# Two sliding-window attention and MLP layers on one core: three units project q, k, v by seven block products, the first unit's feed-forward reads its weights where they were split, attention takes four tokens per instruction

## The chip, the cores and the metric

One core of a Trainium2 chip runs the whole program. The metric is the device time of one execution in microseconds (us): the median of 3 runs of the kernel before is 1144.45 us (1144.21 to 1144.93).

## The reference

The input x is [1, 2048, 640] in fp32. Two layers follow each other with the same weights. Each does

```
x = x + A(layernorm(x));   x = x + B(layernorm(x))
A(y): q, k, v = y @ wqkv (640 x 1920), 32 heads of 20
      token s sees 8 keys: s, s-2, ..., s-14 (masked where negative)
      softmax over the 8 logits / sqrt(20), weighted sum of v, then @ wo (640 x 640)
B(y): h = gelu_tanh(layernorm(y) @ w1 + b1)   (640 x 1536)
      h @ w2 + b2                              (1536 x 640)
```

All products are to be as accurate as fp32; the kernel gets there by splitting each fp32 factor into two fp16 parts, high and low, and adding three of the four products (`PASS`).

## The kernel before

The 2048 tokens are cut into four *units* of 512 (even or odd tokens, first or second half; a partition holds four neighbouring tokens `t`). Two layers make eight units in order, 0 to 7. A unit goes through these stages:

- `layernorm(n, ..., twice=False)`: ScalarE (ACT) forms the statistics and the normalised row y, the high part and, on VectorE (DVE), the low part (L618); the DMA queue transposes each of the four tiles (`dma_transpose`) into a `yT` buffer.
- `qkv(n)`: 16 pieces (4 tokens x 4 head groups `g`), each 5 blocks of 128 rows x 3 passes = 15 matmuls of 480 columns (L648); ACT evicts each piece (L665) and SyncE (SP) writes it to a DRAM buffer `spill`.
- `fetch(G)` and `attention(G)`, 4 groups of heads per unit, G = 0 to 31: q, and k and v with their halo rows, come back from `spill`. DVE does the logits (products L732, sums over 20 L736), the softmax (L741 to L751, the exponential on ACT), the weighted sum (products L758, a tree of sums L766, L770). Each of L732, L736, L758, L766 is issued for two tokens at a time (`EH = 2`), and the two halves alternate in two `pr` buffers. GpSimd (POOL) splits the output for three groups of four, DVE for the fourth (L780).
- `project(n)`: 120 matmuls of 320 columns with wo (L805) onto the residual.
- `layernorm(n, ..., twice=True)`, then `mlp(at, b, t0, t1)`: for each of 12 blocks of 128 hidden columns 15 matmuls (L871), gelu and high part on ACT (L877, L880), low part on DVE (L882), 24 matmuls into five accumulators (L892). Both weight blocks are loaded again from DRAM (`mw`) for each part of `PARTS`.
- The last two units, 6 and 7, share one feed-forward in `pair()`, which already uses seven block products for eight: `sums_of_weights` (L1005, L1018, L1020) and `joint` (L952 to L978) make the sums of weights and of rows on DVE; L1108 and L1073 are its matmuls.

Before any feed-forward can start, all of w1 and w2 is read, split into fp16 parts (L475 on ACT, L476 on DVE) and stored in `mw` (`prep_m`, L517); `mlp` waits for all of it (`split_done`). Unit 0's feed-forward is cut into two parts of two tokens, `(0, 0, 2), (0, 2, 4)`, with matmuls of 256 columns in L871.

The order of all instructions on all engines is fixed when the program is built. `Plan` lists the operations with durations, priorities (lower first), what each needs and gives, and the buffers it uses (`SLOTS`; those in `ORDERED` go to their users in order), plays them through a model of the engines and the DMA queues, and emits each engine's instructions in the order that came out. At run time every engine works off its own list in that order and waits by semaphores. All DMAs but a few are issued by SP, in one such list.

Of the kernel before, what the change touches and what calls it, by code (L numbers as in the profile page):

```python
# [26 lines left out]
REST = D - BANK  # L27

# [3 lines left out]
M = 4  # L32
# [4 lines left out]
EH = 2  # L37

# [32 lines left out]
THROUGH = (("sa", 29),)  # L71
LOP = ((29, -460),)


class Plan:
# [23 lines left out]
    ORDERED = ("qk", "v", "yT", "o", "ohl", "c1", "c2", "hh", "h32", "ev", "raw")  # L99
# [191 lines left out]
def sliding_dilated_then_mlp_kernel(  # L291
# [25 lines left out]
    def many(pool, n, shape, dt, name):  # L317
# [3 lines left out]
             "sy": 4, "sa": 4, "sm": 2, "ln": 3, "ps": 3, "z": 2, "zh": 2, "raw": 2, **{f"acc{i}": 1 for i in range(5)}}  # L321
# [11 lines left out]
        "pr": many(sb, SLOTS["pr"], [P, EH, W, GC], FT, "pr"),  # L333
# [24 lines left out]
    blocks = [("o", k) for k in range(KD)] + [("m", f, i) for f in range(NF) for i in range(2)]  # L358
    through = {name: next(pool for pool, n in THROUGH if i < n) for i, name in enumerate(blocks)}
    split_done = [("lo", k) for k in blocks]  # L360

    def passed(pool):
        return [("lo", k) for k in blocks if through[k] == pool]
# [24 lines left out]
    for i, q in enumerate(("A12", "S1", "A22", "HL")):  # L388
# [4 lines left out]
        "pr": [("o", 2 * NU * NG - 1, a) for a in range(M // EH)] + [("done", 0, i) for i in range(M)],  # L393
# [84 lines left out]
    def prep_q(g, prio):  # L478
# [8 lines left out]
        for i in range(3):  # L487
# [3 lines left out]
            a, v = split(lambda i=i: wq[:, 0, :, g, i], lambda i=i: wq[:, 1, :, g, i], lambda i=i: st(i))  # L491
# [3 lines left out]
    def prep_rows(name, prio, src, hi, lo, use=()):  # L495
        key = (through[name], name)

        def load():
            st = tile_of(*key)
            w = src()  # L500
            nc.sync.dma_start(st.rearrange("p (k c) -> p k c", k=w.shape[1]) if len(w.shape) == 3 else st, w)

        dma(P * D * 4 / 1e3, prio, load, need=[("ev", 0, M - 1, 0)], give=[("st", name)], use=[key],
            packet=4 * P if name[0] == "m" and not name[2] else 4 * D)
        a, v = split(hi, lo, lambda: tile_of(*key))
        act(D, prio, a, need=[("st", name)], give=[("hi", name)], use=[key, *use])
        dve(D, next(p for n, p in LOP if blocks.index(name) < n), v, need=[("hi", name)], give=[("lo", name)], use=[key, *use])

    def prep_o(k, prio):
        prep_rows(("o", k), prio, lambda: A_wo[k * P:(k + 1) * P], lambda: wo[:, 0, k], lambda: wo[:, 1, k])  # L510
# [837 lines left out]
```

## Time and profile before

| | us |
|---|---|
| median of 3 runs | 1144.45 |
| span of the profiled execution | 1146.1 |
| TensorE (PE) matmuls busy in it | 1137.1 |
| DVE busy | 1038.4 |
| ACT busy | 606.6 |
| POOL busy | 113.2 |
| DMA, share of 16 engines | 70% |

The profiled execution's own time is known only by its span, from the first to the last instruction, which lies 1.65 us above the median. Busy time is the union of an engine's instructions; a stage can be bound by another engine than the whole. Matmuls overlap each other, so the time of a stretch of them is read from starts, or from the chain of work, and not from the duration of one.

### The profile page before, as it was taken

How to read it: one execution, taken by the hardware profiler on the slowest of the kernel's cores; microseconds unless marked ns; L12 is line 12 of the kernel's file. 1: busy time of each engine (PE TensorE's matmuls, PEld its weight loads, DVE VectorE, ACT ScalarE, POOL GpSimd, SP SyncE). 2: the span in 40 equal slices, each digit the busy share in tenths (PEclk: the TensorE clock that was granted, in tenths of full speed). 3: DMA queues.
4: the chain of work that ended last, by engine and by line, in shares of the span. 5: the costliest groups of instructions: out<-in, count | busy, mean ns of one | idle time of the engine just before them, and what ended most of it. 6: DMA issues, size and time to landing. Idle time of an engine off the chain costs nothing.

```text
span 1146.1 us, 17470 instructions
## 1 busy us (share of the span) xinstructions
PE 1137.1 (99%) x6812; PEld 628.4 (55%) x6812; DVE 1038.4 (91%) x1028; ACT 606.6 (53%) x1131; POOL 113.2 (10%) x94
## 2 busy tenths in 40 slices
PE   9999999999999999999999999999999999999998
PEld 6444446567565465546555555556455556555476
DVE  7999999999899999999999999999999993847972
ACT  6485336536365275734537662479347445657720
POOL 1010000211111102110112012012111000000000
PEclk9999999999999999999999999999999999999999
DMA  9999998978976477576655965569686555974201
GB/s 318 307 299 266 329 302 244 321 264 244 239 189 232 140 221 213 178 207 198 186 187 176 221 190 164 175 188 192 164 247 183 175 171 156 217 239 122 65 24 69
DMA packets 239791, 235.47 MB, mean 205 GB/s; under 512 B 139020, under 2 KB 195164, under 8 KB 239708
## 3 DMA queue, kind: packets, MB, share of 16 engines
q1 hardware_dynamic: 239708, 234.36, 69.9%
q8 instruction: 53, 0.87, 0.3%
q14 instruction: 30, 0.25, 0.1%
HBM read 157.55 MB, written 44.78 MB: 177 GB/s over the span
## 4 chain that ended last, share of the span: by engine, by line
PE 72%; DVE 3%; DMA 1%; issue 0%; ACT 0%; DVEq 0%
PE acc L892 18%; PE ps L871 17%; PE ps L648 17%; PE ps L805 10%; PE acc L1073 4%; PE ps L1108 3%; PE ps L1073 2%; DMA yT<-w 1%; DVE yT L1020 1%; DVE pr L1005 1%; PE acc L1108 1%; DVE wq L1194 0%; DVE wq L1182 0%; DVE v L1195 0%; DVE xf L1196 0%
## 5 line engine op out<-in xcount | busy, mean ns | idle before, releaser
L648 PE MATMUL ps<-wq,yT 128*128 128x480 f16 (+1 forms) x1950 | 391.0, 363 | 1.5 <-DMA yT<-w 1.1
L648 PEld LDWEIGHTS <-yT 128*128 128x128 f16 x1950 | 189.3, 98 | 200.8 <-DMA yT<-w 1.4
L892 PE MATMUL acc<-c,act 128*128 128x512 f16 (+1 forms) x1728 | 249.3, 299 | 2.3 <-DMA c<-mw 1.6
L871 PE MATMUL ps<-yT,c 128*128 128x512 f16 (+1 forms) x1260 | 247.8, 350 | 0.0
L892 PEld LDWEIGHTS <-act 128*128 128x128 f16 x1728 | 136.1, 98 | 108.8 <-issue 1.9
L871 PEld LDWEIGHTS <-c 128*128 128x128 f16 x1260 | 120.9, 98 | 107.3 <-DMA c<-mw 0.3
L732 DVE TENSOR_TENSOR pr<-qk 128x2560 f32<-128x2560 f32 x64 | 179.5, 2808 | 0.0
L758 DVE TENSOR_TENSOR pr<-sm,v 128x2560 f32<-128x2560 f32 x64 | 179.1, 2818 | 0.3
L736 DVE TENSOR_REDUCE sm<-pr 128x128 f32<-128x2560 f32 x64 | 179.2, 2801 | 0.0
L665 ACT ACTIVATE ev<-ps 128x480 f32<-128x480 f32 x128 | 72.6, 568 | 177.2 <-PE ps L648 157.5
L877 ACT ACTIVATE act<-ps,b 128x512 f32<-128x512 f32 (+1 forms) x84 | 52.4, 624 | 172.9 <-PE ps L871 170.2
L766 DVE TENSOR_TENSOR pr<-pr 128x640 f32<-128x640 f32 (+1 forms) x128 | 143.1, 1150 | 0.3
L805 PE MATMUL ps<-wo,yT 128*128 128x320 f16 x960 | 131.7, 299 | 0.0
L805 PEld LDWEIGHTS <-yT 128*128 128x128 f16 x960 | 93.8, 98 | 37.4
L780 POOL TENSOR_TENSOR ohl<-w,ohl 128x640 f16<-128x640 f32 x24 | 34.9, 1456 | 425.9 <-DVE pr L732 171.6
L882 DVE TENSOR_TENSOR act<-act 128x512 f16<-128x512 f32 (+1 forms) x84 | 51.0, 609 | 16.0 <-ACT act L880 15.9
L587 POOL TENSOR_TENSOR ln<-ln,half 128x2 f32<-128x2 f32 (+1 forms) x31 | 36.2, 1173 | 276.6 <-ACT ln L584 276.6
L625 POOL TENSOR_TENSOR xf<-xf,b 128x640 f32<-128x640 f32 x24 | 37.3, 1558 | 144.6 <-DVE pr L732 58.4
L880 ACT ACTIVATE act<-act 128x512 f16<-128x512 f32 (+1 forms) x84 | 47.5, 565 | 3.4 <-PE acc L892 1.5
L610 ACT ACTIVATE w<-xf,ln 128x640 f32<-128x640 f32 x53 | 47.5, 909 | 2.7 <-DVE w L618 2.1
L570 ACT ACTIVATE junk<-xf 128x640 f16<-128x640 f32 x57 | 41.8, 733 | 12.9 <-DVE xf L814 8.0
L618 DVE TENSOR_TENSOR w<-w,w 128x640 f16<-128x640 f32 x56 | 45.7, 830 | 2.1 <-ACT w L616 2.1
(200 smaller groups left out, 984.1 us busy)
## 6 DMA issues: line engine op xcount, KB each, us to landing
c<-mw SPq DMA_DIRECT2D x174, 320.0 KB, 3.6
spill<-ev SPq DMA_DIRECT2D x64, 480.0 KB, 3.6
qk<-spill SPq DMA_DIRECT2D x32, 880.0 KB, 6.0
v<-spill SPq DMA_DIRECT2D x32, 880.0 KB, 5.3
qk<-spill SPq DMA_DIRECT2D x32, 320.0 KB, 3.6
act<-in_B_w_dram SPq DMA_DIRECT2D x24, 320.0 KB, 4.9
mw<-c SPq DMA_DIRECT2D x24, 320.0 KB, 4.7
pr<-in_B_w_dram SPq DMA_DIRECT2D x24, 320.0 KB, 4.1
```

The costliest lines, as they stand in the source:

```text
L648: nc.tensor.matmul(ps, transposed(yk)[:, a * KD + k, t * P:(t + 1) * P], wq[:, b, k, g, i0:i1], start=first and j == 0, stop=last and j == ...
L665: act(3 * GC, -400 + n, lambda i=i, pk=pk, ek=ek: nc.scalar.activation(tile_of(*ek)[:, :, i], tile_of(*pk)[:, :3 * GC].rearrange("p (a c) ...
L732: nc.vector.tensor_mul(tile_of(*pk), w[:, HALO + m + t0:HALO + m + t0 + EH, None, :].to_broadcast([P, EH, W, GC]), windows(w, t0, [GC, W], ...
L736: dve(E, G - 0.7, lambda pk=pk, t0=t0: nc.vector.tensor_reduce(lg(t0, t0 + EH).rearrange("p t w h -> p (t w h)"), tile_of(*pk).rearrange(" ...
L758: nc.vector.tensor_mul(tile_of(*vk).rearrange("p t w (h d) -> p t (w h) d", d=DH), lg(t0, t0 + EH).rearrange("p t w h -> p t (w h)")[:, :, ...
L766: dve(EH * w * GC, G - 0.9, lambda vk=vk, w=w: nc.vector.tensor_add(tile_of(*vk)[:, :, 0:w], tile_of(*vk)[:, :, 0:w], tile_of(*vk)[:, :, w ...
L805: nc.tensor.matmul(tile_of(*pk)[:, :D // 2], transposed(yk)[:, a * KD + k, t * P:(t + 1) * P], wo[:, b, k, c * D // 2:(c + 1) * D // 2], s ...
L871: nc.tensor.matmul(tile_of(*pk)[:, :nt], tile_of(*ck)[:, a, k * P:(k + 1) * P], transposed(yk)[:, c * KD + k, t0 * P:t1 * P], start=i == 0 ...
L877: act(nt, -430, lambda pk=pk, h32=h32, e=e: nc.scalar.activation(tile_of(*h32)[:, :nt], tile_of(*pk)[:, :nt], AF.Gelu_apprx_tanh, bias=b1[ ...
L882: dve(nt, -1000, lambda h32=h32, hk=hk: nc.vector.tensor_sub(tile_of(*hk)[:, 1, :nt], tile_of(*h32)[:, :nt], tile_of(*hk)[:, 0, :nt]), nee ...
L892: nc.tensor.matmul(accs[k][:, c0:c0 + n], tile_of(*hk)[:, a, (i - t0) * P:(i - t0 + 1) * P], tile_of(*wk)[:, c, w0:w0 + n], start=first, s ...
L1073: nc.tensor.matmul(tile_of(*to(i))[:, :HALF], hl()[:, a, i * P:(i + 1) * P], row(c), start=start and (a, c) == PASS[0], stop=(a, c) == PAS ...
```

## The change

- **Units 5, 6, 7** (`SEVEN`) project by `qkv7` in place of `qkv`. Two tiles of 128 tokens (`b`) and two head groups (`p`) make a 2 x 2 block product; four of the five row blocks are multiplied by seven products (the fifth in the ordinary way). A block (p, b) takes 6 + 9 + 9 + 6 + 9 + 6 + 9 = 54 matmuls of 480 columns for 60. Its accumulators A, B, Cb are the three `ps` banks; ACT copies A to B after P1 and evicts the running sums between products (`keep`), and DVE adds two of them at the end (`ea`).
- Its factors: `sums_of_rows` makes sums of normalised rows on DVE and four splits and transposes for each b (two 128 x 640 before); the added rows lie in the memory of `wq` that the factors leave. `factors` makes sums of the weights, once, in four rounds after unit 4's projection, and stores two sets `ws` in DRAM. `wq` holds one set; after a unit's first two blocks the other set is loaded over it, and units alternate which is first (`half_first`).
- **Unit 0's feed-forward** is one part of four tokens. It reads the split weights in the `c1`/`c2` buffer where they were split (`("c1", ("prep", e))`); they are also stored for later parts. Raw weights are staged in `c1`/`c2` too, and `split_done` is gone. The projection of unit 3 gets a later priority.
- **Attention** issues each of L732, L736, L758, L766, L770 once for four tokens. `pr` is one buffer `[P, W, M, GC]` of which each step uses both halves; the logits lie as (t h w), so that the maximum and the sum over w read neighbours; L736 writes and L758 reads them by key (`by_key`, a step of 8 words).

```diff
-PARTS = [(0, 0, 2), (0, 2, 4)] + [(b, 0, 4) for b in range(1, 2 * NU - 2)]
+PARTS = [(b, 0, 4) for b in range(0, 2 * NU - 2)]
+SEVEN = (5, 6, 7)
...
-    wq = sb.tile([P, 2, KD, NG, 3, GC], HT, name="wq")
+    wq = sb.tile([P, NG, KD, 2, C], HT, name="wq")
...
+    def sums_of_rows(n, prio, name, yk, lk, col):
...
+            def sum1(yks=yks):
+                y1 = tile_of(*yks[1])
+                nc.vector.tensor_add(y1[:, :KQ], y1[:, :KQ], y1[:, KQ:2 * KQ])
+            def sums(yks=yks):
+                y0, y1 = (tile_of(*k) for k in yks)
+                nc.vector.tensor_sub(y0[:, :KQ], y1[:, :KQ], y0[:, :KQ])
+                nc.vector.tensor_sub(y0[:, KQ:2 * KQ], y0[:, KQ:2 * KQ], y0[:, :KQ])
+                nc.vector.tensor_sub(y0[:, 2 * KQ:], y0[:, 2 * KQ:], y1[:, 2 * KQ:])
+                nc.vector.tensor_sub(y1[:, KQ:2 * KQ], y1[:, KQ:2 * KQ], y0[:, :KQ])
...
+    def factors():
...
+                    for to, a, b in ((b11, b12, b11), (b12, b22, b12), (b22, b22, b11), (b21, b21, b22)):
+                        nc.vector.tensor_sub(to, a, b)
...
+    def qkv7(n):
...
+            step("P1", A, [("A11", "B11")], True, 6, before)
+            act(C, -401 + n, lambda A=A, B=B: nc.scalar.activation(tile_of(*B)[:, :C], tile_of(*A)[:, :C], AF.Copy),
+                need=[("P1", n, p, b)], give=[("cp", n, p, b)], use=[A, B])
+            step("P5", Cb, [("S1", "T1"), ("A2r", "R1")], True, 5, before)
+            keep("sP5", Cb, at(tk, 1), "P5", [tk])
+            step("P2", A, [("A12", "B21"), ("A1r", "R0")], False, 4, [("cp", n, p, b)], [("qkvp", n, t0, g0)])
+            keep("C11", A, at(e0, 0), "P2", [e0])
+            step("P6", B, [("S2", "T2")], False, 3, [("cp", n, p, b)])
+            keep("su2", B, at(tk, 0), "P6", [tk])
+            step("P3", Cb, [("S4", "B22"), ("D", "R1")], False, 2, [("sP5", n, p, b)], [("qkvp", n, t0, g1)])
+            step("P7", B, [("S3", "T3")], False, 1, [("su2", n, p, b)], [("qkvp", n, t1, g1)])
+            keep("su3", B, at(e1, 1), "P7", [e1])
+            keep("C12", Cb, at(e1, 0), "P3", [e1])
+            step("P4", B, [("A22", "T4"), ("A2r", "R0")], False, 0, [("su3", n, p, b)], [("qkvp", n, t1, g0)])
+            keep("C21", B, at(e0, 1), "P4", [e0])
+            dve(2 * C, -420 + n, ..., give=[("ea", n, p, b)], use=[tk, e1])
...
+            if s == 1:
+                last = {"B11": "P1", "T1": "P5", "R1": "P3", "B21": "P2", "R0": "P4", "T2": "P6", "B22": "P3", "T3": "P7", "T4": "P4"}
+                for q, w in last.items():
+                    size = 1 if q[0] == "R" else 2
+                    dma(..., lambda q=q, p=p: nc.sync.dma_start(flat(home(q)), ws[1 - p, q]),
+                        need=[(w, n, p, b), *stored(1 - p, q), *stored(p, q)], give=[("sw", n, q)], packet=size * 4 * C)
...
-                prio, done = -500 + n + 0.01 * k, ("qkvp", n, t, g)
+                prio, done = (-500 if n != NU - 1 else 13) + n + 0.01 * k, ("qkvp", n, t, g)
...
-        E = EH * W * GC
+        E = m * W * GC
...
+        dve(E, G - 0.6, qk, need=[("inq", G), ("ink", G)], give=[("qk", G)], use=[wk, *pk, sk])
+        dve(E, G - 0.7, lambda: nc.vector.tensor_reduce(by_key(), heads(), axis=AX.X, op=OP.add),
+            need=[("qk", G)], give=[("lg", G)], use=[*pk, sk])
...
+        dve(E, G - 0.85, lambda: nc.vector.tensor_mul(
+            heads(), by_key()[:, :, :, None].to_broadcast([P, W, m * GH, DH]), windows(tile_of(*vw), [DH, m * GH], [1, DH])),
+            need=[("at", G), ("inv", G)], give=[("pv", G)], use=[vw, sk, *vk])
...
-            ck, wk = ("c1", j), ("c2", j)
+            ck, wk = (("c1", j), ("c2", j)) if at else (("c1", ("prep", e)), ("c2", ("prep", e)))
+            cgot, wgot = ([k] if at else [("lo", ("m", e, i))] for i, k in enumerate((ck, wk)))
...
-            mm(3 * KD * nt, 15, j - 1.0 - AHEAD, inner, need=[*ready, ck, *split_done] + [("hhi", j - 2)] * (e > 1), give=[("hp", j)],
+            mm(3 * KD * nt, 15, j - 1.0 - AHEAD, inner, need=[*ready, *cgot] + [("hhi", j - 2)] * (e > 1), give=[("hp", j)],
```

## Rows read from the trace of the kernel before

**Rows 1.** The page's first part: busy us, share of the span, instructions.

```profile
PE 1137.1 (99%) x6812; PEld 628.4 (55%) x6812; DVE 1038.4 (91%) x1028; ACT 606.6 (53%) x1131; POOL 113.2 (10%) x94
```

**Rows 2.** Stretches: their length, then PE, PEld, DVE, ACT, POOL busy, clock, DMA, GB/s.

```profile
200.50:945.60 745.10, 741.68 (x4508) 409.31 (x4507) 728.21 (x624) 393.97 (x740) 94.68 (x68) 1.00 0.70 202
...
229.20:257.80 28.60, 26.61 (x207) 19.04 (x206) 27.77 (x25) 10.62 (x20) 3.06 (x2) 0.94 0.78 265
...
1060.00:1088.70 28.70, 28.64 (x145) 13.97 (x143) 28.23 (x47) 20.21 (x35) 0.00 (x0) 1.00 0.22 65
...
1117.30:1146.00 28.70, 25.36 (x187) 18.03 (x185) 6.94 (x16) 0.00 (x0) 0.00 (x0) 0.98 0.20 69
```

**Rows 3.** The chain that ended last: start us, us, engine, tile, line, matmuls.

```profile
319.92 12.15 PE ps L648 x60
...
333.16 1.64 PE ps L871 x15
...
352.70 3.24 PE ps L871 x15
...
375.43 24.30 PE ps L648 x120
...
1103.40 9.92 PE acc L1073 x73
```

**Rows 4.** PE in order of time: start us, us, instruction, count, [idle before].

```profile
239.97 1.05 PE L892 MATMUL acc<-c,act 128*128 128x512 f16 x4 [1.26 <-DMA c<-mw]
240.81 3.16 PE L871 MATMUL ps<-yT,c 128*128 128x256 f16 x15
...
244.90 1.80 PE L871 MATMUL ps<-yT,c 128*128 128x256 f16 x15
...
958.24 16.46 PE L805 MATMUL ps<-wo,yT 128*128 128x320 f16 x120
```

**Rows 5.** Groups of DVE and ACT instructions by shape: busy us, mean ns | idle before.

```profile
L758 DVE TENSOR_TENSOR pr<-sm,v 128x2560 f32<-128x2560 f32 x64 | 179.1, 2818 | 0.3
L766 DVE TENSOR_TENSOR pr<-pr 128x1280 f32<-128x1280 f32 x64 | 93.8, 1483 | 0.1
L665 ACT ACTIVATE ev<-ps 128x480 f32<-128x480 f32 x128 | 72.6, 568 | 177.2 <-PE ps L648 157.5 <-issue 11.9 <-DMA act<-in_B_w_dram 4.9
L766 DVE TENSOR_TENSOR pr<-pr 128x640 f32<-128x640 f32 x64 | 51.1, 817 | 0.2
L749 DVE TENSOR_REDUCE sm<-sm 128x32 f32<-128x256 f32 x32 | 19.5, 611 | 6.3 <-ACT sm L747 6.2
L744 DVE TENSOR_REDUCE sm<-sm 128x32 f32<-128x256 f32 x32 | 19.4, 607 | 0.2
L745 DVE TENSOR_TENSOR sm<-sm 128x256 f32<-128x256 f32 x32 | 13.4, 420 | 0.3
```

**Rows 6.** DVE in order of time.

```profile
54.06 0.62 DVE L749 TENSOR_REDUCE sm<-sm 128x32 f32<-128x256 f32 x1 [0.48 <-ACT sm L747]
...
298.37 5.56 DVE L758 TENSOR_TENSOR pr<-sm,v 128x2560 f32<-128x2560 f32 x2
...
835.84 5.55 DVE L732 TENSOR_TENSOR pr<-qk 128x2560 f32<-128x2560 f32 x2
...
945.62 0.82 DVE L780 TENSOR_TENSOR ohl<-w,ohl 128x640 f16<-128x640 f32 x1 [0.80 <-ACT ohl L777]
```

**Rows 7.** DMA issues on SP of joint's transposes: ns min/median/max, first and last start.

```profile
L978 SPq DMA_TRANSPOSE wq<-xf x4: 1447/1602/3221, 980.7 to 994.9; - x4
...
DMA to landing us min/median/max: 4.0/4.3/6.4
```

**Rows 8.** The page's DMA issues: out<-in, count, KB each, us to landing.

```profile
c<-mw SPq DMA_DIRECT2D x174, 320.0 KB, 3.6
...
act<-in_B_w_dram SPq DMA_DIRECT2D x24, 320.0 KB, 4.9
mw<-c SPq DMA_DIRECT2D x24, 320.0 KB, 4.7
```

More of the change, by code (lines that the diff above doesn't have):

```diff
@@ L320, in sliding_dilated_then_mlp_kernel @@
     SLOTS = {"qk": 1, "v": 1, "ev": 3, "yT": 3, "ohl": 1, "pr": 2, "c1": 3, "c2": 3, "hh": 3, "h32": 2, "y": 2, "w": 5,
[L321 removed]
+             "sa": 4, "sm": 2, "ln": 3, "ps": 3, "z": 2, "zh": 2, "raw": 2, "ax": 1, "ts": 1, **{f"acc{i}": 1 for i in range(5)}}
     plan = Plan(SLOTS)
@@ L356, in transposed @@
         return tile_of(*key).rearrange("p (k c) -> p k c", k=2 * KD)
[L358 to L363, printed above, removed]
-    wq = sb.tile([P, 2, KD, NG, 3, GC], HT, name="wq")
+    wq = sb.tile([P, NG, KD, 2, C], HT, name="wq")
     wo = sb.tile([P, 2, KD, D], HT, name="wo")
-    wq_flat = wq.rearrange("p a k g i c -> p (a k g i c)").bitcast(FT)
+    wq_flat = wq.rearrange("p g k a c -> p (g k a c)").bitcast(FT)
     wo_flat = wo.rearrange("p a k c -> p (a k c)").bitcast(FT)
@@ L392, in sliding_dilated_then_mlp_kernel @@
         "wq": [("qkvp", last_n, t, g) for t in range(M) for g in range(NG)],
-        "pr": [("o", 2 * NU * NG - 1, a) for a in range(M // EH)] + [("done", 0, i) for i in range(M)],
+        "pr": [("o", 2 * NU * NG - 1)] + [("done", 0, i) for i in range(M)],
         "wo": [("wop", last_n, t, c) for t in range(M) for c in range(2)],
@@ L598, in layernorm @@
             kept.append((lk, col))
+        if not twice and n in SEVEN:
+            return sums_of_rows(n, prio, name, yk, lk, col)
         for t in range(m):
@@ L635, in qkv @@
         yk = ("yT", ("a", n))
-        halves = [(g, b) for g in range(NG) for b in range(2)] if n == 0 else [(g, b) for b in range(2) for g in range(NG)]
+        halves = [(g, b) for p in range(2) for b in range(2) for g in (2 - 2 * p, 3 - 2 * p)] if n == SEVEN[0] - 1 else [
+            (g, b) for g in range(NG) for b in range(2)] if n == 0 else [(g, b) for b in range(2) for g in range(NG)]
+        chain = []
         for k, (g, b) in enumerate(halves):
@@ L654, in qkv @@
                        need=([("yT", ("a", n), t, a, i) for a in range(2) for i in range(2)] if n == 0 else [("yT", ("a", n), t)])
-                       + [("wq", g, i) for i in range(3)], give=[done], use=[pk, yk])
+                       + [("wq", g, i) for i in range(3)] + chain, give=[done], use=[pk, yk])
+                    chain = [done] if n == SEVEN[0] - 1 else []
                 else:
@@ L739, in attention, with heads, qk @@
-        last = [("lg", G, a) for a in range(NE)]
+        def heads():
+            return pr.rearrange("p w t (h d) -> p w (t h) d", d=DH)
+        pk, vk = ([("pr", (G, j, i)) for i in range(2)] for j in range(2))
+        def qk():
+            w = tile_of(*wk)
+            nc.vector.tensor_mul(pr.rearrange("p w t c -> p w (t c)"),
+                                 w[:, HALO + m:HALO + 2 * m].rearrange("p t c -> p (t c)")[:, None, :].to_broadcast([P, W, m * GC]),
+                                 windows(w, [1, m * GC]))
@@ L774, in hi @@
+        last = ("pv", G)
+        for w in (4, 2):
+            dve(m * w * GC, G - 0.9, lambda w=w: nc.vector.tensor_add(pr[:, 0:w], pr[:, 0:w], pr[:, w:2 * w]),
+                need=[last], give=[("ad", G, w)], use=vk)
+            last = ("ad", G, w)
+        dve(m * GC, G - 0.9, lambda: nc.vector.tensor_add(ot(), pr[:, 0], pr[:, 1]), need=[last], give=[("o", G)], use=[*vk, ok])
         def hi():
@@ L905, in mlp @@
         mm(2 * REST * len(tiles), 2 * len(tiles), j, lambda: [outer(i, PASS[:2], [rest(i)]) for i in tiles],
-           need=[("hhi", j), wk, *before], give=[("outh", b, e, ("rest", at))], use=[wk, hk, last])
+           need=[("hhi", j), *wgot, *before], give=[("outh", b, e, ("rest", at))], use=[wk, hk, last])
         mm(REST * len(tiles), len(tiles), j - 0.2, lambda: [outer(i, PASS[2:], [rest(i)]) for i in tiles],
```

280 lines of the change are left out of this document (208 added, 72 removed).

## The prediction, made before the changed kernel was run

> **What bounds the kernel now.** Read the page's busy times first: PE 1137.1 of a span of 1146.1 us, DVE 1038.4, ACT 606.6 [rows 1]. PE looks like the whole answer, but it can be busy because another engine leaves it just enough other work, so the second view is the stretches: from 200.5 to 945.6 us PE is busy 741.7 of 745.1 and DVE 728.2, that is 98%, idle 16.9 [rows 2]. The third view is the chain: there PE runs at full rate, 60 matmuls of 480 columns in 12.15 us (0.2025 each), 15 of 512 in 3.24 (0.216), 73 of 320 in 9.92 (0.136) [rows 3]. So PE can lose time only by having fewer columns; its idle time is 9 us in all, 3.3 of them behind the last matmul [rows 2].
>
> DVE is the second bound. The last attention ends at 945.62 + 0.82 = 946.4 us [rows 6]. What must follow it in any case: unit 7's output product, its second layernorm, the sums of rows in `joint` and their transposes, the last issued at 994.9 and landing 4.3 us later, at 999.2 [rows 7]: 52.8 us. Then everything in `pair` that needs these rows: 39 x 6 = 234 matmuls of 512 columns, 234 x 0.216 = 50.5 us, and six of the second layer's products, 6 x 6 x 4 x 3 = 432 of 320, 432 x 0.136 = 58.7 us: 109.2. Then 3.3 us. Sum: 946.4 + 52.8 + 109.2 + 3.3 = 1111.7. The rest up to 1146.1, 34.4 us, is PE work that fits anywhere in the tail. So there are two bounds: PE's total, at 1146.1, and DVE up to the last attention, at 1111.7. The change moves both, in opposite directions.
>
> **PE: what it removes.** A unit takes 4 x 54 = 216 matmuls of 480 columns for 240; three units save 72 x 0.2025 = 14.6 us [rows 3]. Unit 0's feed-forward takes 12 times 15 matmuls of 512 columns at 3.24 us for 24 times 15 of 256 at 1.64 [rows 3]: 39.4 - 38.9 = 0.5 saved. L892 has the same matmuls as before. PE's bound: 1146.1 - 15.1 = 1131.0.
>
> Unit 0's feed-forward now waits for weights on another path. Before, PE stood 1.26 us there for a reload, and the next 15 matmuls of 256 columns, in the slice whose clock reads 0.94, took 3.16 us for 1.80 [rows 2, 4]: 2.6 us that a resident weight spares. Against it, each of the 12 blocks must be loaded (4.9 us), split (the like of L766's 640 elements: 0.8 on each of ACT and DVE) and stored (4.7) in three buffers, the raw block in one and the split in the next [rows 5, 8]: 6.5 + 6.3 = 12.8 us of buffer time per block, over 3 buffers 4.3 us, below the 6.5 us of PE work per block (twice 3.24: L892 has as many columns as L871). If each split also stands twice behind a DVE instruction of 5.5 us it is 7.9 per block, 1.4 x 12 = 17 us late. What covers that is unit 3's projection, 48.6 us of PE work that is put off for it. I take nothing for this part, between -2.6 and +17.
>
> **DVE: what it removes.** One element costs (1483 - 817) / 640 = 1.041 ns; a second L758 right behind the first adds 5.56 - 2.82 = 2.74 us for 2560 elements, so an instruction costs 0.076 us over its elements [rows 5, 6]. Per group 12 instructions become 6: 6 x 0.076 x 32 = 14.6 us. The maximum and the sum over keys take 0.607 and 0.611 us for 256 elements read 8 words apart, the subtraction of as many neighbours 0.420 [rows 5]; read as neighbours, 0.19 x 64 = 12.1 us less. With 12 fewer L882 (0.9): -27.6.
>
> **DVE: what it adds.** Sums of rows, per b: five sums of 1152 elements in all, low parts of 640 x 3 + 256 in four instructions for 1280 in two; 2048 elements and 7 instructions more, 2.13 + 0.53 = 2.66; x 6 = 16.0. Sums of weights, per round 4 x 480 + 1440 + 480 elements in 6 instructions, 4.45; x 4 = 17.8. The final `ea`, 960 elements, 1.075; x 12 = 12.9. Together +46.7, net +19.1, all ahead of the last attention. DVE's bound moves from 1111.7 to 1130.8.
>
> **Costed at nothing.** ACT gets some 8 copies per block for 4 (0.57 us each [rows 5]; 12 x 4 x 0.57 = 27 us) and 14 us of splits; at 606.6 busy it hides them, unless one is late for PE (a rival below). The four rounds of `factors` hang behind unit 4's projection, which ends at 399.7 [rows 3]. Unit 7's attention lasts from 835.84 to 946.4, 110.6 us [rows 6]; at that length for each, unit 5's starts near 615. Those 215 us cover the rounds; without cover each would cost its load, 5 us, its sums and its splits, some 12 us. The sums of rows need the projection before to be done and add five transposes, about 1.6 us of SP each [rows 7], some 12 us in all ahead of unit 6's and 7's projection. Unit 7's is the one without slack: its first attention instruction at 835.84 [rows 6] ran as its q and k landed. But DVE comes to it 19 us later than before, and PE some 10 earlier. SP's later entries, the loads for attention, stand behind these transposes; that is in the same 12 us. DMA: two loads of 24 blocks of 320 KB for unit 0 go (15.7 MB [rows 8]), 7.9 MB of factors written, 3.9 read raw and 3 x 3.9 swapped in come: +8 of 235 MB. Longer DVE instructions hold back POOL, and L882 for which PE waits, by up to 2.7 us more; PE's lead of one block, 6.5 us, covers this. One `pr` buffer in place of two lets less of two groups overlap. Where nothing fills the wait for the exponential it is 0.48 us [rows 6], 6.2 in all before [rows 5]; at worst 32 x 0.48 = 15.4, so 9 more, at best nothing; I take 2.
>
> **The sum.** PE 1131.0, DVE 1130.8 + 2 = 1132.8: for once the same. PE's work that fits anywhere in the tail is 34.4 + 52.8 - 16.3 (the output product, 120 x 0.136; its row of 16.46 us ends in an overlap [rows 4]) = 70.9 us before. Until the last attention PE now has 15.1 us less to do and 21 us more time, so 36 of these are used up by then, and the 34.8 left have to fill the 36.5 us between the last attention and unit 7's rows: almost exactly. Two bounds that meet cost a little over the later one: I take a span of 1133.7, which is 12.4 under 1146.1. The span of before lies 1.65 over the median, so the median is forecast at 1132. Its own range: 1127 to 1138.
>
> **Rivals.**
> *PE alone decides.* DVE's idle 16.9 us shrink and unit 0's waits go: 1131.0 - 2.6 - 1.65 = 1127, down to 1124 if the two other idle microseconds go too. For: the waits of before are in that part. Against: DVE's sum is at the same place.
>
> *The seven products wait for ACT.* P4 needs P7 evicted; P7's drain and a 0.57 us copy [rows 5] make about 0.95 us, covered only by the next block's P1 of 6 x 0.2025 = 1.2. If no cover is there: 12 x 0.95 = 11.4 us, and as much again if the copy behind P1 is late as well: 1143 to 1155. Against it: `pair` has the same chain of products and evictions and PE is busy 28.64 of 28.70 us there [rows 2]. If it is part exposed, 1138 to 1143.
>
> *The other side: DVE pays for the step of 8 words.* L758 now reads the logits, and L736 writes them, 8 words apart. If that costs what it costs L744, 0.73 ns an element ((607 - 420) / 256), on all 5120 elements of L758, it is 3.7 us a group and 120 in all: about 1250. If it costs once per logit, each of which is held for 20 elements, it is 0.19 us a group, 6 us in all, and as much for the writes: 1138 to 1144. From 0.45 us a group on (14 us) it is slower than before. The rows speak for the small end: L758 holds each logit for 20 elements already and runs at full rate (2818 ns for 2560). On this the Trainium skill's "Vector Engine (DVE) Microarchitecture Reference", section "5.2 Measured stream behaviour on trn2", says that a port keeps its full rate only where elements come in runs of at least two adjacent words, and that a hop at every element costs about 0.65 cycle. The strided L744 agrees in size; whether a held word counts as a run no run here shows, and by the rule at one hop per logit it would be 0.17 us a group.
>
> *Swapped factors come late.* 3.9 MB per unit must land in two blocks' time, 21.9 us: 179 GB/s on top of the 202 that the queue moves on the mean [rows 2]. If they get half of what they need, the second half of a unit is some 15 us late; the attention of the first two groups, some 50 us, covers it, but not if both halves are wanted early. Price without cover: 3 x 5 to 3 x 15 us on DVE, 1145 to 1175.
>
> **Chances.** Forecast 0.58; PE alone (under 1127) 0.10; products part exposed, faster still, 0.10; about no change (exposed products or both small DVE costs) 0.09; slower 0.13, of which the step of 8 words or the single buffer 0.06, products 0.03, swaps or unit 0's weights 0.04. Medians of this kernel tell 0.2% (2.3 us) from no change: faster than 1142.2 0.78, within 0.09, slower than 1146.7 0.13. The range for 8 of 10 leaves a little of the first rival and most of the slower ones out: 1123 to 1147.
>
> **What would show it.** Right: in the new trace PE stays above 99% busy; a block of seven takes 10.9 us; L732, L736, L758 take about 5.41 to 5.5 us once per group; the reductions over keys 0.42; the last attention ends near 965, and PE is idle a few us at most between there and unit 7's rows. Wrong: gaps before P4 or P2; gaps of PE or a lower clock in unit 0's feed-forward; L758 above 5.6 us; DVE waiting for q and k at a unit's start; an end of attention beyond 975.

## The result, and the profile after

The changed kernel takes 1146.64 us (median of 8 runs, 1145.3 to 1150.05) beside 1144.38 of the kernel before on the same chip: ratio 1.0021, 95% interval 1.0012 to 1.0031. It is slower by 0.2%, where 1132 was forecast. The profiled execution has a span of 1148.1 us (its own time is 1149.85); the span of the forecast was 1133.7, so 14.4 us are to be found. Both profiled executions are slow ones of their kernel, 3.2 us above the median here and some 3.4 before, so the 14.4 compares like with like, but most profiles below lie near their medians and have the end of the last attention some 3 us earlier for that alone: in before_pool_short, whose median is that of the kernel before, it stands at 942.7 and not at 946.4. The wide range of the forecast, 1123 to 1147, still holds the result at its edge; the direction was wrong.

First the page of the changed kernel, its busy line, to be held against [rows 1]:

```profile
PE 1125.1 (98%) x6560; PEld 604.1 (53%) x6560; DVE 1072.3 (93%) x901; ACT 630.2 (55%) x1163; POOL 144.4 (13%) x94
```

PE did lose its work: 12.0 us less busy, 252 matmuls fewer recorded. But it is idle 23.0 us for 9.0, DVE has 33.9 us more and POOL, which the change gives nothing to do, 31.2 us more.

Next the end of the last attention on DVE, in order of time (columns as in [rows 6]), and the stretches behind it (length, then PE, PEld, DVE, ACT, POOL, clock, DMA share, GB/s):

```profile
973.75 0.83 DVE L1002 TENSOR_TENSOR ohl<-w,ohl 128x640 f16<-128x640 f32 x1 [0.80 <-ACT ohl L999]
```

```profile
974.60:1029.80 55.20, 50.62 (x315) 29.57 (x312) 37.45 (x64) 41.33 (x76) 4.47 (x2) 1.00 0.92 214
1029.80:1148.10 118.30, 111.79 (x678) 66.22 (x678) 84.23 (x148) 51.26 (x82) 0.00 (x0) 1.00 0.28 85
```

The attention ends at 974.6; the forecast's sum puts it at 1132.8 - 3.3 - 109.2 - 52.8 = 967.5. Unit 7's rows have landed at 1029.8, 55.2 us later (52.8 forecast); from there to the end it takes 118.3 (112.5, and 0.9 for the two bounds that meet). So 7.1 + 2.4 + 4.9 = 14.4: half of the miss lies ahead of the last attention and half behind it.

DVE's groups up to 974.6, by shape (busy us, mean ns | idle before), beside [rows 5]:

```profile
L965 DVE TENSOR_TENSOR pr<-qk 128x5120 f32<-128x5120 f32 x32 | 176.6, 5519 | 1.0 <-DMA qk<-spill 0.7
L986 DVE TENSOR_TENSOR pr<-sm,v 128x5120 f32<-128x5120 f32 x32 | 176.5, 5516 | 0.4
L991 DVE TENSOR_TENSOR pr<-pr 128x2560 f32<-128x2560 f32 x32 | 91.3, 2854 | 0.2
L991 DVE TENSOR_TENSOR pr<-pr 128x1280 f32<-128x1280 f32 x32 | 50.7, 1583 | 0.2
L834 DVE TENSOR_TENSOR ev<-ev,ev 128x960 f32<-128x960 f32 x12 | 15.0, 1246 | 0.1
L982 DVE TENSOR_REDUCE sm<-sm 128x32 f32<-128x256 f32 x32 | 13.0, 409 | 1.1 <-ACT sm L980 1.0
L977 DVE TENSOR_REDUCE sm<-sm 128x32 f32<-128x256 f32 x32 | 12.9, 403 | 0.2
```

The reductions over keys fell to 0.41, as forecast. L965 and L986 have their forecast length. But the second L991 (1280 elements) takes 1583 ns for the 1483 that this shape had before, and `ea` 1246 for the 1075 of the forecast. In order of time most of the excess is not spread: single instructions are 1.1 to 1.4 us longer than their like. Such a place, DVE first and then POOL:

```profile
810.94 5.48 DVE L986 TENSOR_TENSOR pr<-sm,v 128x5120 f32<-128x5120 f32 x1
816.34 2.03 DVE L1105 TENSOR_TENSOR act<-act 128x512 f16<-128x512 f32 x1
```

```profile
811.16 6.66 POOL L624 TENSOR_TENSOR xf<-xf,b 128x640 f32<-128x640 f32 x1 [0.77 <-DVE sm L978]
```

POOL's addition of b2, 1.54 us elsewhere, begins 0.2 us into DVE's product and ends 1.4 us after it: it stood all that time. Then L1105, 0.68 us elsewhere, takes 2.03: it stood until POOL was done at 817.82. Counting every DVE instruction that is over 0.25 us longer than the median of its line and shape, the changed kernel has 14 ahead of the last attention, each with a POOL instruction of L1002 or L624 beside it, 15.7 us longer together; the kernel before has 2, 1.7 us. (Against the shortest of the like it is the 16.2 and 1.8 that an expectation below names.) On POOL's side the groups of the changed kernel, then of the kernel before:

```profile
L1002 POOL TENSOR_TENSOR ohl<-w,ohl 128x640 f16<-128x640 f32 x24 | 49.2, 2049 | 401.1 <-DVE pr L965 202.2 <-DVE pr L986 148.7 <-ACT ps L820 15.5
L624 POOL TENSOR_TENSOR xf<-xf,b 128x640 f32<-128x640 f32 x24 | 41.8, 1758 | 32.1 <-DVE w L617 10.6 <-ACT ln L581 10.5 <-DVE sm L983 8.6
L584 POOL TENSOR_TENSOR ln<-ln,half 128x2 f32<-128x2 f32 x26 | 39.6, 1523 | 369.8 <-ACT ln L581 369.8
L584 POOL TENSOR_TENSOR ln<-ln,half 128x1 f32<-128x1 f32 x5 | 9.2, 1839 | 40.8 <-ACT ln L581 40.8
```

```profile
L625 POOL TENSOR_TENSOR xf<-xf,b 128x640 f32<-128x640 f32 x24 | 37.3, 1558 | 144.6 <-DVE pr L732 58.4 <-DVE ohl L780 28.3 <-DVE act L882 26.6
L780 POOL TENSOR_TENSOR ohl<-w,ohl 128x640 f16<-128x640 f32 x24 | 34.9, 1456 | 425.9 <-DVE pr L732 171.6 <-DVE sm L745 95.3 <-ACT ohl L777 63.1
L587 POOL TENSOR_TENSOR ln<-ln,half 128x2 f32<-128x2 f32 x26 | 29.8, 1150 | 230.4 <-ACT ln L584 230.4
```

L780, which is L1002 in the new kernel, was released most often by the first product (L732), in front of DVE's reduction. The first product (L965) still ends half of the idle time before L1002, but now a good third ends with the weighted product (`<-DVE pr L986`), and what DVE does next is the first sum L991, with two inputs again.

### The profile page after: what moved, and what is told of

Read it like the earlier page. It is cut to its first block, busy times and chain, and to the rows that moved or that the text cites. A ratio compares the mean times of both kernels' runs of the same rounds, so it can differ in the third digit from the quotient of the medians.

```text
span 1148.1 us, 16909 instructions
## 1 busy us (share of the span) xinstructions
PE 1125.1 (98%) x6560; PEld 604.1 (53%) x6560; DVE 1072.3 (93%) x901; ACT 630.2 (55%) x1163; POOL 144.4 (13%) x94
## 4 chain that ended last, share of the span: by engine, by line
PE 32%; DVE 19%; issue 6%; ACT 5%; DMA 2%; POOL 1%; POOLq 0%; SPq 0%; DVEq 0%; ACTq 0%
PE ps L1094 8%; PE acc L1115 8%; PE ps L802 6%; PE ps L1027 4%; DVE pr L965 3%; PE acc L1296 3%; DVE sm L970 3%; DVE pr L991 2%; PE ps L1296 2%; DVE pr L986 2%; DVE pr L1228 2%; PE ps L1331 1%; DVE wq L736 1%; DMA wq<-ws0T 1%; DVE act L1105 1%
## 5 line engine op out<-in xcount | busy, mean ns | idle before, releaser
L874 PE MATMUL ps<-wq,yT 128*128 128x480 f16 (+1 forms) x1230 | 244.4, 361 | 0.4 <-DVE yT L536 0.2
L1094 PE MATMUL ps<-yT,c 128*128 128x512 f16 x1080 | 243.1, 379 | 1.0 <-DMA yT<-w 1.0
L1115 PEld LDWEIGHTS <-act 128*128 128x128 f16 x1728 | 136.2, 98 | 113.2 <-issue 3.3
L965 DVE TENSOR_TENSOR pr<-qk 128x5120 f32<-128x5120 f32 x32 | 176.6, 5519 | 1.0 <-DMA qk<-spill 0.7
L986 DVE TENSOR_TENSOR pr<-sm,v 128x5120 f32<-128x5120 f32 x32 | 176.5, 5516 | 0.4
L970 DVE TENSOR_REDUCE sm<-pr 128x256 f32<-128x5120 f32 x32 | 175.1, 5472 | 0.1
L991 DVE TENSOR_TENSOR pr<-pr 128x2560 f32<-128x2560 f32 x64 | 142.0, 2219 | 0.4
L1027 PE MATMUL ps<-wo,yT 128*128 128x320 f16 x960 | 134.4, 301 | 4.4 <-DMA yT<-ohl 2.6
L1027 PEld LDWEIGHTS <-yT 128*128 128x128 f16 x960 | 94.2, 98 | 43.7 <-DMA yT<-ohl 3.6
L1100 ACT ACTIVATE act<-ps,b 128x512 f32<-128x512 f32 x72 | 49.1, 682 | 106.2 <-PE ps L1094 105.5
L584 POOL TENSOR_TENSOR ln<-ln,half 128x2 f32<-128x2 f32 (+1 forms) x31 | 48.7, 1574 | 410.7 <-ACT ln L581 410.7
L1002 POOL TENSOR_TENSOR ohl<-w,ohl 128x640 f16<-128x640 f32 x24 | 49.2, 2049 | 401.1 <-DVE pr L965 202.2
L892 ACT ACTIVATE ev<-ps 128x480 f32<-128x480 f32 x80 | 45.1, 567 | 99.1 <-PE ps L874 94.9
L802 PE MATMUL ps<-wq,yT 128*128 128x480 f16 x396 | 84.3, 366 | 0.0
L802 PE MATMUL ps<-wq 128*128 128x480 f16 x252 | 53.8, 366 | 2.9 <-ACT ev L811 2.1
L1105 DVE TENSOR_TENSOR act<-act 128x512 f16<-128x512 f32 x72 | 51.0, 716 | 1.0 <-ACT act L1103 0.8
```

What stands on the lines that cost most here:

```text
L802: nc.tensor.matmul(ps, r(x_, j), w[:, j, y_], start=start and i == 0, stop=i == len(todo) - 1, skip_group_check=True)
L874: nc.tensor.matmul(ps, transposed(yk)[:, a * KD + k, t * P:(t + 1) * P], wq[:, g, k, b, i0 * GC:i1 * GC], start=first and j == 0, stop=las ...
L965: nc.vector.tensor_mul(pr.rearrange("p w t c -> p w (t c)"), w[:, HALO + m:HALO + 2 * m].rearrange("p t c -> p (t c)")[:, None, :].to_broa ...
L970: dve(E, G - 0.7, lambda: nc.vector.tensor_reduce(by_key(), heads(), axis=AX.X, op=OP.add), need=[("qk", G)], give=[("lg", G)], use=[*pk, sk])
L986: dve(E, G - 0.85, lambda: nc.vector.tensor_mul(heads(), by_key()[:, :, :, None].to_broadcast([P, W, m * GH, DH]), windows(tile_of(*vw), [ ...
L991: dve(m * w * GC, G - 0.9, lambda w=w: nc.vector.tensor_add(pr[:, 0:w], pr[:, 0:w], pr[:, w:2 * w]), need=[last], give=[("ad", G, w)], use=vk)
```

## The experiments

Each run shares a chip with runs of the kernel before (medians 1144.5 to 1144.9), and its ratio is to these. All but no_seven keep the order of instructions of the kernel that they edit (under_reduce and none_beside move POOL's alone): the order is worked out from durations, and a version with other durations would get another order throughout. "Attention end" and "stretched" (as counted above) are from each profile.

**pool_short.** POOL's low part and its b2 on a few columns.

```diff
-            eng.tensor_sub(tile_of(*hk)[:, :, 1, g * GC:(g + 1) * GC], ot(), hi())
+            eng.tensor_sub(tile_of(*hk)[:, :, 1, g * GC:g * GC + c], ot()[:, :, :c], hi()[:, :, :c])   # c = 2 on POOL
-                ... nc.gpsimd.tensor_add(x[u][:, t], x[u][:, t], b2),
+                ... nc.gpsimd.tensor_add(x[u][:, t, :8], x[u][:, t, :8], b2[:, :8]),
```

> The changed kernel with its order of instructions kept; GpSimd's 24 splits of the attention output (L1002) and 24 additions of b2 (L624) work on 8 columns in place of 640, so their results are incomplete; in unit 0 ACT fills the low part once more (3 copies). Theory 1 (DVE decides, and GpSimd's long operations make DVE's instructions beneath them 1.2 us longer, 14 times in the profiled run, 16 us): the stretched DVE instructions vanish, the last attention ends 12 to 16 us earlier (near 960), the time falls by 9 to 14 us, to 1133 to 1138. Theory 2 (PE decides: its waits in the seven products and in the tail): within 2 us of the changed kernel, 1145 to 1148. Theory 3 (DVE decides, but through its own added instructions alone): within 3 us, 1144 to 1148.

1139.76 us, ratio 0.9957 (0.9942 to 0.9972), 7 us under the changed kernel, between the ranges of the theories and 1.8 above the first; no stretched instruction; the attention ends at 964.0, 10.6 earlier, of which some 7 are the edit's. POOL still waits, but no DVE instruction waits for it. Its power L584 takes up to 7.3 us, and in all 48.4 us (45.1 + 3.3) where the changed kernel has 48.8 (39.6 and 9.2 for its two shapes):

```profile
L584 POOL TENSOR_TENSOR ln<-ln,half 128x2 f32<-128x2 f32 x26 | 45.1, 1734 | 380.0 <-ACT ln L581 380.0
L584 POOL TENSOR_TENSOR ln<-ln,half 128x1 f32<-128x1 f32 x5 | 3.3, 665 | 39.8 <-ACT ln L581 39.8
```

So the gain does not come from shorter waits of the power; what these waits cost is open.

**before_pool_short.** The same cut in the kernel before.

> The kernel before with the same cut as in pool_short: POOL's low part of the attention's output (L780) on 2 of 16 columns per group and b2 on 8 of 640, order kept; output wrong in that part. In the kernel before only 2 DVE instructions were stretched (1.8 us), against 14 (16.2 us) in the changed one. Theory (the changed kernel's loss is that its 5.4 us instructions of DVE and POOL's work hold each other up): the same cut gains at most 2.5 us here, 1142 to 1145, where it gained 7 in the changed kernel. Rival (POOL's work costs any version of this kernel the same): 1136 to 1139.

1144.46 us, ratio 0.9995 (0.9986 to 1.0003): the cut is worth nothing there. Of the two kernels POOL's work costs only the changed one.

**ea_short.**

```diff
-                *(tile_of(*k).rearrange("p a t c -> p (a t c)") for k in (e1, e1, tk))),
+                *(tile_of(*k).rearrange("p a t c -> p (a t c)")[:, :8] for k in (e1, e1, tk))),
```

> The changed kernel, order kept; the 12 additions at the end of the seven products (ea, 960 elements) add 8 elements only, so two of eight pieces of q, k, v of a block are wrong. DVE has 12 x 1.0 = 12 us less to do ahead of the last attention, PE the same. Theory 1 and 3 (DVE decides): 8 to 12 us less, 1135 to 1139. Theory 2 (PE decides): within 2 us, 1145 to 1148.

1151.04 us, ratio 1.0056 (1.0036 to 1.0075). This is above every range named. DVE is busy 11.3 us less and idle 12.5 us more; the attention ends at 975.8. Why less work makes it slower, and not only no faster, is open.

**mm_short.** P6 and P7 with one matmul for six.

```diff
+                    todo = todo[:1] if what in ("P6", "P7") else todo
```

> The changed kernel, order kept; products P6 and P7 of each block take 1 matmul for 6, so q, k, v of units 5 to 7 are wrong. PE has 12 x 10 x 0.2025 = 24.3 us less to do, all ahead of the last attention, DVE the same. Theory 1 and 3 (DVE decides): within 3 us of the changed kernel, 1143 to 1148. Theory 2 (PE decides): 15 to 24 us less, 1122 to 1132.

1149.54 us, ratio 1.0041 (1.0026 to 1.0056): 24 us of PE work less, no gain, and above both ranges; PE is idle 19.9 us between 530 and 900. A part of the cut is lost to PE's clock: it reads 0.94, 0.88 and 0.94 in the slices from 688.7, 803.5 and 975.6 (28.7 us each, with PE idle 4.0, 4.0 and 3.3 us), which is some 7 us of PE work (an estimate: the missing shares times 28.7). Neither sum alone sets the time.

**no_seven.** Unit 0's feed-forward and the four-token attention without the block products, order worked out anew.

```diff
-SEVEN = (5, 6, 7)
+SEVEN = ()
```

> The changed kernel without the seven products (SEVEN is empty: units 5 to 7 project as before; no sums of weights), the order planned anew; four tokens at once and unit 0's feed-forward as changed. By counts DVE has 46.7 us less to do than in the changed kernel and 19 to 28 less than in the kernel before, PE 14.6 more than in the changed one. Theory 1 and 3: PE decides again, and its work is that of the kernel before less 0.5: 1141 to 1146, so about as before, and the last attention ends by 945. Theory 2: the waits of the seven products go, PE the same: 1141 to 1146 as well, so this run tells whether the other two parts of the change cost or give anything by themselves: each us below 1144 is theirs, and above 1146 they cost.

1147.21 us, ratio 1.0018 (1.0009 to 1.0028). That is 1.2 above the range expected, so the other two parts cost some 2.4 us by themselves; where is not traced. DVE has 15 stretched instructions (16.7 us) here too, so they don't need the block products. But the attention ends at 950.8 and DVE is idle 48.0 us up to there (20.8 of it until q and k land), where PE is busy 944.6: this leaves room to hide them. That they cost only where DVE sets the end is argued from this and not shown.

**pow_on_dve, halves, halves_pow_on_dve.** Is it the length of L965 and L986, or POOL's tiny power behind them?

```diff
-            pool(0.5, prio, lambda t0=t0, t1=t1: nc.gpsimd.tensor_tensor(
-                col(2)[:, t0:t1], col(2)[:, t0:t1], half[:, t0:t1], op=OP.pow),
+            pool(0.5, prio, lambda t0=t0, t1=t1: nc.vector.tensor_scalar(
+                col(2)[:, t0:t1], col(2)[:, t0:t1], 0.001, 20.0, op0=OP.mult, op1=OP.add),
```

```diff
-            nc.vector.tensor_mul(pr.rearrange("p w t c -> p w (t c)"), ...)
+            for i in range(2):
+                nc.vector.tensor_mul(pr[:, i * W // 2:(i + 1) * W // 2].rearrange("p w t c -> p w (t c)"), ...)
```

> The changed kernel, order kept, with POOL's 32 tiny powers of the layernorm (L584, up to 5.6 us behind a long DVE instruction) taken off POOL: DVE does a multiply and an add on the same few columns instead, so the normalisation's scale is wrong. POOL's L1002 and L624 stay. Theory: the wait of POOL's power behind DVE, which ACT and then PE hang on, is one of two parts of the loss: 2 to 5 us less than the changed kernel, 1142 to 1144.5. Rival (only the stretch of DVE's instructions under L1002 and L624 costs): no change, 1146 to 1148.

> The changed kernel, order kept, with each of the two long products of a group (L965, L986) issued as two instructions of 2560 elements, as in the kernel before; all else as in the changed kernel, the output too. By the difference of 76 ns per instruction DVE has 64 x 0.076 = 4.9 us more to do. Theory (length of the instruction is what holds POOL up): POOL's waits and the stretched instructions shrink, so in spite of the 4.9 us it is no slower than the changed kernel: 1141 to 1146. Rival (DVE's sum decides): 1150 to 1152.

> Both edits, halves and pow_on_dve, together (scale of the normalisation wrong), order kept. Theory: 1139 to 1144, below either alone. Rival (DVE's sum decides): 1150 to 1152, as halves.

1159.07 us (1.0126, 1.0109 to 1.0142), 1154.24 (1.0077, 1.0061 to 1.0093) and 1165.73 (1.0173, 1.0154 to 1.0192). My reasons fell in all three. In pow_on_dve the substitute waits in DVE's own list:

```profile
DVE ln L584 <- ACT ln L581: 14.2, 4, 11.8
```

(DVE's waits: total us, times, longest.) So it says nothing on what POOL's power costs. In halves 14 instructions are stretched as before, 15.5 us: POOL's L1002 is released by the end of L986, and whether that was one instruction or two, L991 follows. So halving the length removes none of them; what stands on either side of the release is tested next. The 4.9 us of added work came on top, and 3 us more, of which 2.5 lie behind the last attention (176.0 us for 173.5); their cause is open.

**under_reduce.** After the order is fixed, POOL's long instructions are moved to the next reduction L970, as far as their result may wait; output unchanged.

```diff
+    for o in [o for o in order if o["eng"] == "pool" and o["pair"] and o["dur"] > 1]:
...
+            if order[c]["give"][0][0] == "lg" and len(here) < 3 and a < stop:
+                o["behind"] = order[a]
+                if a > i:
+                    order.insert(a + 1, o)
+                    del order[i]
+                break
```

> The changed kernel, order of DVE, PE and ACT kept, output the same: 8 of POOL's 48 long instructions that were released in front of a two-input DVE instruction wait for the next reduction over the head (L970) instead; 7 whose result is wanted before that stay. Theory (POOL beside two-input instructions is the loss): the 14 stretched DVE instructions go down to about 7, the time to 1140 to 1144, below the changed kernel's 1146.6. Rival (pool_short gained because POOL had less to do at all): no change, 1146 to 1148.

1142.74 us, ratio 0.9985 (0.9976 to 0.9993); 7 stretched, 7.5 us; attention end 967.2. Nothing was left out here, so these 3.9 us hang on where POOL works, not on how much.

**none_beside.** The seven that stayed go to DVE.

```diff
+        if dves[dves.index(o["behind"]) + 1]["give"][0][0] != "lg":
+            del o["behind"]
+            on_dve.add(o["give"][0])
```

> As under_reduce, and the 7 that stayed are done by DVE at their place (7 x 0.75 = 5 us more DVE work, output the same): POOL has no long instruction beside a two-input one. Theory: at most 2 stretched DVE instructions, POOL's power waits less; 1139 to 1143, no slower than under_reduce although DVE has more to do. Rival (DVE's sum decides): under_reduce + 5.

1141.58 us, ratio 0.9972 (0.996 to 0.9983): below both kernels, with the whole computation. No stretched instruction, the attention ends at 965.1 although DVE has seven instructions more. Its POOL groups, then its two long products on DVE and the second L991 (here L993), back at the length of before:

```profile
L626 POOL TENSOR_TENSOR xf<-xf,b 128x640 f32<-128x640 f32 x22 | 33.5, 1546 | 39.9 <-DVE ev L836 29.4 <-DVE sm L979 10.5
L1004 POOL TENSOR_TENSOR ohl<-w,ohl 128x640 f16<-128x640 f32 x19 | 26.6, 1402 | 354.8 <-DVE sm L985 98.3 <-DVE sm L984 47.6 <-DVE ohl L1004 37.8
```

```profile
L988 DVE TENSOR_TENSOR pr<-sm,v 128x5120 f32<-128x5120 f32 x32 | 175.5, 5484 | 0.4
L967 DVE TENSOR_TENSOR pr<-qk 128x5120 f32<-128x5120 f32 x32 | 175.4, 5482 | 0.2
L993 DVE TENSOR_TENSOR pr<-pr 128x1280 f32<-128x1280 f32 x32 | 47.5, 1484 | 0.2
```

Behind the attention nothing has changed: 173.8 us to the end, 173.5 in the changed kernel.

**pool_tail_short.** That rest: pool_short with the last units' sums of weights cut.

```diff
             for to, a, b in (...):
-                nc.vector.tensor_sub(to, a, b)
+                nc.vector.tensor_sub(to[:, :8], a[:, :8], b[:, :8])
```

> pool_short, with the sums of weights of the last two units (L1233, 12 x 4 instructions of up to 320 elements, about 24 us of DVE, and a part of L1246 and L1248) cut to 8 columns; output wrong. For the remainder that pool_short left against the forecast: from the start of unit 7's output product to unit 7's rows it takes 47.5 us, and 41.0 in the kernel before, where none of these sums lay between. Theory (these sums hold up the layernorm and the sums of rows on DVE and ACT): the 47.5 become 41 to 44, the time is 3 to 6 us under pool_short's 1139.8. Rival (the path is held by ACT's evictions for PE, not by the sums): no more than 1.5 us under it.

1133.94 us, ratio 0.9905 (0.9892 to 0.9919), 5.8 under pool_short. From the output product to the rows it takes 45.0 us, not the 41 to 44 expected. The two stretches, pool_short first:

```profile
964.00:1019.50 55.50, 51.17 (x319) 29.84 (x316) 37.41 (x65) 41.14 (x76) 4.48 (x2) 1.00 0.92 214
1019.50:1137.90 118.40, 111.79 (x678) 66.23 (x678) 84.37 (x148) 51.36 (x83) 0.00 (x0) 1.00 0.28 85
```

```profile
962.80:1015.20 52.40, 50.65 (x318) 29.85 (x316) 30.30 (x66) 40.06 (x77) 1.95 (x2) 1.00 0.96 226
1015.20:1131.40 116.20, 111.31 (x678) 66.22 (x678) 71.68 (x146) 48.03 (x82) 0.00 (x0) 1.00 0.28 86
```

With DVE 7 us less busy in the first, it is 3.1 us shorter, and the second 2.2: the sums hold up the rows and PE's last products, together 5.3 of the 173.9 (the cut takes their work away, and not only their place in the order).

**pool_ea_short, pool_mm_short, pool_ea_mm_short.** With POOL out of the way, which sum decides?

> pool_short and ea_short together (the last sum of each block of seven on 8 of 960 elements; output wrong): DVE has 11 us less to do than in pool_short. Theory (with POOL out of the way DVE's sum up to the last attention decides, as the forecast had it): the attention ends 8 to 11 us earlier, near 954, and the time falls until PE's total is the bound: 1130 to 1136. Rival (waits of DVE for ACT and PE take it back, as they did in ea_short): attention end 960 or later, 1138 to 1141.

> pool_short with P6 and P7 of the blocks of seven on 1 matmul for 6 and `ea` unchanged (24.3 us less of PE before the last attention; output wrong). Theory (two bounds in force at once: PE's work and DVE's up to the last attention): DVE's stays, so the attention ends at 960 to 964 and the time is 1136 to 1140, PE's saving becomes idle time before 964. Rival (PE alone holds DVE back): the attention ends 10 us or more earlier, 1130 or less.

> pool_short, ea_short and mm_short together: 11 us less for DVE and 24 us less for PE before the last attention (output wrong). Theory (two bounds at once): now the attention ends 8 to 11 us earlier than pool_short's 964.0, near 954, and the time is 1128 to 1132. Rival (ACT holds DVE back, whatever PE has to do): the attention ends at 962 or later, 1137 to 1141.

pool_ea_short 1142.51 us (0.9981, 0.9972 to 0.999), attention end 965.2; pool_mm_short 1136.98 (0.9934, 0.9921 to 0.9946), 961.3; both 1135.05 (0.9916, 0.9903 to 0.993), 957.8. Only pool_mm_short lies in the range of its theory; pool_ea_short is 2.8 us slower than pool_short and above both of its ranges, and the run with both cuts lies between its two. DVE's waits in pool_ea_short, then with both:

```profile
DVE w L617 <- ACT w L615: 11.0, 8, 3.5
DVE act L1110 <- ACT act L1108: 9.9, 8, 2.5
```

```profile
DVE w L617 <- ACT w L615: 9.6, 8, 3.5
DVE act L1111 <- ACT act L1109: 3.2, 5, 1.2
```

In pool_short these two are 5.4 and 3.2 us up to the last attention. So DVE's freed 11 us became waits: 9.9 us for the feed-forward's ACT, which waits for PE, and these fall back to 3.2 when PE has less to do. With POOL away PE does hold DVE, as pool_mm_short's theory of two bounds in force at once has it; the attention's end moves 6.2 us with both cuts and 2.7 with PE's alone, though the clock reads 0.94 in three slices of pool_mm_short and in one with both cuts, some 5 and 2 us of PE work by the same estimate. Expected were 8 to 11: the waits for the normalised rows (L617) stay, and what holds these is open.

## Why the prediction was wrong

**The step that failed first** is the one costed at nothing: "Longer DVE instructions hold back POOL, and L882 for which PE waits, by up to 2.7 us more; PE's lead of one block, 6.5 us, covers this." It priced the wait of POOL (the longest addition took 6.66 us for 1.54), and asked who waits for POOL; it left out that DVE waits for POOL in turn, on the engine with the later of the forecast's two bounds. That is 15.7 us for 1.7, nearly all in single waits of 1.1 to 1.4. What it costs in the end is less: 6.9 us by pool_short, 5.1 by none_beside, which pays for seven instructions more, and the control shows none of it in the kernel before. The 6.9 are about the 7.1 us by which the attention ends too late: DVE's work up to there grew by 37.2 us (913.5 to 950.7) for the 19.1 forecast, of which the stretches are 14.0, and its idle time fell by 9.0 where 2 more were taken, so 18.1 - 11.0 = 7.1. That the idle time took up so much was not foreseen. With the stretches gone the attention ends at 964.0 and 965.1; counted from 942.7 in place of 946.4, the forecast's 967.5 would be 963.8.

On this the Trainium skill's "SBUF — State Buffer", section "Who interferes with whom", says that a DVE instruction with two SBUF inputs contends with a GpSimd instruction that reads SBUF, that the pair of ports which the two engines share is an exclusive lock, that issue order decides who blocks, and that `tensor_reduce` never contends on trn2. The rows at 811 and 816 show the waiting on both sides, and in none_beside the POOL instructions that were moved under reductions take their shortest time (1402 ns).

Why the order of before had so little of this and the new one did, is argued from the source and not tested: `Plan` is written with such a rule (`PAIRS`, the kinds of DVE instruction that bar POOL), but the change's own sums (`ea`, `rs`, `rs2`) are not in that list, and POOL is allowed to slip in behind `pv`. I read POOL's waits of before and not where each would be released after.

**The second step** is the tail: "the 34.8 left have to fill the 36.5 us between the last attention and unit 7's rows: almost exactly". The work was there (PE is busy 162.4 us behind the attention). But PE is idle 11.1 us there, 6.6 with the sums cut, and 3.5 in the kernel before:

```profile
946.40:999.20 52.80, 52.80 (x344) 30.40 (x342) 32.78 (x58) 32.61 (x61) 2.64 (x2) 1.00 0.80 181
999.20:1146.10 146.90, 143.39 (x868) 83.60 (x865) 92.11 (x160) 66.61 (x108) 0.00 (x0) 1.00 0.35 109
```

`pair`'s products moved into this stretch (90 matmuls of 512 columns of L1331 behind the start of unit 7's output product in pool_short, 6 of their like before), and these want sums of weights from DVE and evictions from ACT, while both make unit 7's rows. The waits of PE in the changed kernel, of which the first of L1027 lies in unit 0 and those of L1331, 4.6 us in all and 4.0 of them for ACT, are new:

```profile
PE ps L1027 <- DMA yT<-ohl: 2.6, 1, 2.6
PE ps L802 <- ACT ev L811: 2.1, 2, 1.7
PE acc L1115 <- DVE xf L1159: 2.0, 2, 1.2
PE ps L1331 <- ACT ev L1352: 1.7, 1, 1.7
PE ps L1027 <- ACT ps L1039: 1.6, 1, 1.6
...
PE ps L1331 <- ACT wq L1403: 1.1, 2, 0.7
...
PE ps L802 <- DMA wq<-ws0T: 0.8, 2, 0.5
...
PE ps L1331 <- ACT xf L1400: 0.7, 1, 0.7
PE ps L1331 <- DVE xf L1409: 0.6, 1, 0.6
PE ps L1331 <- ACT v L1352: 0.5, 1, 0.5
```

Forecast 166.2 us from the attention to the end, measured 173.5, with the sums cut 168.6. Of the 7.3 too many 5.3 are theirs; the other 2 are not taken apart. With POOL's share and the sums gone the time is 1133.94, within 2 of the forecast: these two interactions between engines make up nearly all of the miss. The agreement does not show that the frame of two separate bounds held: pool_ea_short takes 11 us of work from DVE alone and is slower.

**Point by point.** PE's saving: a block of seven takes 54 matmuls in 10.93 us (710.50 to 721.43 in the trace), as worked out. DVE's terms, each instruction counted up to the start of the next: attention saves 19.7 us for 26.7; the stretches in it are 8.1 us, 1.0 before, so the step itself was right. Sums of weights 18.9 for 17.8, sums of rows 17.1 for 16.0 (1.1 of it stretch), `ea` 14.0 for 12.9 (1.2 of it stretch). The feed-forward's low parts (L882, now L1105) were forecast 0.9 down and are 5.4 up, 2.6 of it stretch: all 72 now come ahead of the last attention, where 6 of 60 stood behind it. The single `pr` buffer: taken at +2; DVE waits 1.1 us for the exponential in all, 6.3 before [rows 5]: a gain, where "at best nothing" was allowed for. Of the marks named beforehand, PE's share failed (98%, not above 99%), and so did the attention's end: 974.6 where near 965 was to show the forecast right, though just inside the 975 that was to show it wrong. Unit 0's feed-forward: PE waits 0.8 us there and the clock stays at 1.00; a lower one, 0.94, now stands at 143.5 to 172.2, behind the 2.6 us for which PE waits at unit 0's output product, for the one of before at 229 [rows 2].

**The rivals.** Seven products waiting for ACT: 2.1 us in all, refuted. Swapped factors late: 0.8 us, refuted. The step of 8 words: in none_beside, which has no stretch, L988 with the step takes 5484 ns and L967 of the same size without it 5482; reading words 8 apart, each held for 20 elements, cost nothing here. The 0.17 us a group that the prediction works out from the Trainium skill's "Vector Engine (DVE) Microarchitecture Reference", section "5.2 Measured stream behaviour on trn2", does not show. PE alone: 24 us less of its work gave nothing (mm_short). The mechanism that decided was not among the rivals; its place was seen and priced at nothing.

## What to carry to other kernels

An engine that shares something with the busiest one belongs in the busiest one's sum: list each GpSimd instruction that reads SBUF, see what VectorE does right behind its release, and give it a place under a reduction, which was worth 4 to 5 us here. When a change adds kinds of instruction, look whether the rule that keeps the two apart knows them. And where two bounds are brought level, the stretch in which the spare work of one covered the other is the next to look at: ask not only how much work is left for it, but what that work asks of the engines it is to cover.

## What was not expected of the hardware

A POOL instruction of 2 elements per partition (L584) takes 0.69 us where nothing bars it and was seen at 5.6 us in the changed kernel and 7.3 in pool_short: the profile counts the time that it stands as busy, so POOL's rise from 113.2 to 144.4 us, with the same 94 instructions, was waiting and no work. In the same way DVE's wait for POOL appears as a longer instruction (L1105 2.03 us for 0.68) and in no view of waits; it is found only by comparing an instruction with its like.
